# Smaller transfers for streamed weights: half a block each for Q, K, V and one row group each for the output weights

## The chip, the cores and the metric

The kernel runs on one core of one Trainium2 chip. The metric is device time in microseconds (us), the time of one execution as the device measures it. A profile of one execution and a trace of its instructions, semaphores and DMA packets belong to each kernel. In the lines of profiles PE is TensorE's matmuls, PEld its weight loads, DVE VectorE, ACT ScalarE, POOL GpSimd and SPq the queue of transfers that SyncE issues; L751 is line 751 of that run's kernel, so the same statement has another number in another run.

## The reference, cut to what matters

The program normalises x, runs layer A, adds it, normalises, runs layer B, adds it, and does all that once more. Layer A is a chain: 64 segments of 32 tokens, each of which starts from 8 memory rows that the segment before has produced. So the segments cannot be run side by side, and each one needs all four weight matrices again (32 heads of 192).

```python
for s in range(n_seg):                       # 2048 / 32 = 64 segments, in order
    xs = x[:, s * seg_len:(s + 1) * seg_len, :].copy()
    h = jnp.concatenate([mem, xs], axis=1)   # 8 memory rows + 32 tokens
    q = jnp.einsum('btd,dhe->bhte', h, Wq)
    k = jnp.einsum('btd,dhe->bhte', h, Wk)
    v = jnp.einsum('btd,dhe->bhte', h, Wv)
    scores = jnp.einsum('bhqe,bhke->bhqk', q, k) * scale
    # ... mask, softmax
    o = jnp.einsum('bhqk,bhke->bhqe', p, v)
    o = jnp.einsum('bhte,hed->btd', o, Wo)
    mem = o[:, :M, :].copy()                 # the next segment waits for this
    outs.append(o[:, M:, :])
```

## The kernel before

The kernel does not keep all weights in on-chip memory. A segment works in four rounds of 8 heads. Most Q, K, V blocks are resident (`res`); 10 blocks (3 of Q, 3 of K, 4 of V) have one slot each, which holds the block of round 0 or of round 3. The output weights of rounds 1 and 2 are resident (`wo_mid`), those of rounds 0 and 3 share `wo_end`. The order of rounds turns around from segment to segment, so that a slot is loaded only once a segment: as soon as the first round has read a slot, the block of the last round is fetched into it. All these loads are issued by SyncE, in program order.

```python
SLOTS = {"Q": 3, "K": 3, "V": 4}
PW = 1536                                     # columns of one block (8 heads x 192)

def load_slot(m, r, b):
    if holds.get((m, b)) != r:
        holds[m, b] = r
        nc.sync.dma_start(out=slot[m, b][:], in_=wview[m][:, b, PW * r:PW * r + PW])

def load_wo(r, into=None):
    t = into if into is not None else wo_end[:, :] if r in (0, 3) else wo_mid[:, 7680 * (r - 1):7680 * r]
    for k in range(4):
        nc.sync.dma_start(out=t[:, 1920 * k:1920 * k + 1920].rearrange("p (c m) -> p c m", m=640),
                          in_=wov[:, 12 * r + 3 * k:12 * r + 3 * k + 3, :])

def project(hT, ps, m, n, s, steps):          # round n of segment s: Q, K or V
    # ... for each block b of the round: four matmuls, then, in the first round:
        if n == 0 and b >= KC - ns:
            load_slot(m, order[NR - 1], b)    # the last round's block into the slot just read

def wo_round(W, r, OT, cs, first, last):      # output weights, 12 row groups c
    w = wo_end[:, :] if r in (0, 3) else wo_mid[:, 7680 * (r - 1):7680 * r]
    for c in cs:
        for g in range(4):
            nc.tensor.matmul(W[32 * g:32 * g + 32, 0:160], lhsT=OT[c // 6][:, c % 6, 8:40],
                             rhs=w[:, 640 * c + 160 * g:640 * c + 160 * g + 160], ...)

# in the chain, one segment s:
for n, r in enumerate(order):
    # ... project Q, K, V of round n; attention and wo_round of round n - 1
        if n == 1:
            load_wo(order[NR - 1])            # wo_end has been read by the first round
# ... after the four rounds:
keep_busy(idle, 4)
O, OT = attend(E, NR - 1)
keep_busy(idle, 2)
attend_rest(O, OT, otb, order[NR - 1])
wo_round(W, order[NR - 1], OT, range(12), False, True)   # the last round of output weights
keep_busy(idle, 3)
if s + 1 < NSEG:
    wt = ...                                  # VectorE: the memory rows out of W,
    nc.vector.transpose(out=wt[:, :, :], in_=W[:, 0:160].rearrange("p (j b) -> p b j", b=KC))
    nc.vector.tensor_copy(out=hT[:, :, 0:8], in_=wt[:, :, 0:8])   # input of the next segment
```

The softmax here doesn't subtract the row's maximum and nothing guards it: scores larger than these inputs give would overflow.

## Time and profile before

| | before |
|---|---|
| median of 3 runs | 4353.34 us (4347.0 to 4354.64) |
| TensorE busy, share of the span | 85% |
| layer A's two chains, 128 segments | 72% of the span, 24.5 us a segment (3135.6 / 128; the prediction's 24.9 divides by 126) |
| streamed a segment | 10 blocks of 384 KB and 4 pieces of 480 KB of output weights, 5.9 MB |
| TensorE's gaps after a fetch of its instructions, both chains | 274 us |

The prediction reads the main views. Three more are needed for the comparison later. First the order of time of SyncE's DMA queue in the segment that starts at 914.4 us (columns: start, length, engine and line, what goes where, how many in a row):

```profile
914.77 1.29 SPq L522 DMA_DIRECT2D wslotQ<-in_A_Wq_dram  x3
916.16 1.33 SPq L522 DMA_DIRECT2D wslotK<-in_A_Wk_dram  x3
917.59 2.02 SPq L522 DMA_DIRECT2D wslotV<-in_A_Wv_dram  x4
922.18 4.62 SPq L535 DMA_DIRECT2D wo_end<-in_A_Wo_dram  x4
```

The last output weights are issued 12.4 us into the segment (922.18 + 4.62 - 914.40).

Second, two of TensorE's groups (columns after the count: busy us, mean ns of one, then idle us just before them and what ended most of it):

```profile
L681 PE MATMUL ps_qk<-w_res,hT 128*32 128x384 bf16 x14336 | 804.8, 334 | 51.0 <-issue 48.0
...
L751 PE MATMUL ps_w<-wo_end,OT 128*32 128x160 bf16 x12288 | 290.5, 235 | 30.2 <-issue 15.9
```

The first are matmuls on resident weights, the second those on `wo_end`.

### The profile page before, as it was taken

The numbers are of one execution on the slowest core, as the hardware profiler recorded it, in microseconds if no ns is written. First come the engines' busy times: TensorE is split into PE (matmuls) and PEld (weight loads), VectorE is DVE, ScalarE is ACT, GpSimd is POOL, SyncE is SP. The second block draws the span as 40 slices with busy tenths as digits, with TensorE's granted clock in tenths as the row PEclk, the third lists the DMA queues.
The fourth block names the chain that finished last, engine by engine and source line by source line (L and its number), as shares of the span: only waits on it lengthen the run. The fifth ranks groups of instructions, "written<-read, shape, count | busy, mean of one in ns | idle before, by whom it ended". The sixth has DMA issues, their size and how long they took to land. (4 is left out here: it accounts for less than half of the span.)

```text
span 4350.8 us, 181511 instructions
## 1 busy us (share of the span) xinstructions
PE 3683.1 (85%) x77592; PEld 2223.0 (51%) x77608; DVE 2248.2 (52%) x5570; ACT 2024.4 (47%) x4973; POOL 1800.7 (41%) x5269
## 2 busy tenths in 40 slices
PE   5888888888888888869869888888888888888698
PEld 4645555555555555535347455555555555555353
DVE  4245555555555555536732455555555555554464
ACT  1245555555555555525412455555555555555152
POOL 1035555555555555430000355555555555553300
PEclk9989999999999999979989899999999999999798
DMA  7777777677677677740076876777777777777200
GB/s 258 214 264 271 254 274 259 247 268 257 247 261 262 239 275 258 273 126 1 31 248 193 280 269 240 273 259 258 276 250 271 251 262 271 252 266 272 84 1 25
DMA packets 613364, 983.28 MB, mean 226 GB/s; under 512 B 145098, under 2 KB 424650, under 8 KB 612554
## 3 DMA queue, kind: packets, MB, share of 16 engines
q1 hardware_dynamic: 459498, 861.74, 54.5%
q0 software_dynamic: 68224, 60.56, 4.6%
q10 hardware_dynamic: 84832, 49.36, 4.1%
q8 instruction: 609, 9.98, 0.9%
q14 instruction: 201, 1.65, 0.1%
HBM read 903.16 MB, written 68.16 MB: 223 GB/s over the span
## 5 line engine op out<-in xcount | busy, mean ns | idle before, releaser
L681 PEld LDWEIGHTS <-hT 128*32 128x32 bf16 x30720 | 785.9, 98 | 596.4 <-issue 217.7
L681 PE MATMUL ps_qk<-w_res,hT 128*32 128x384 bf16 x14336 | 804.8, 334 | 51.0 <-issue 48.0
L666 POOL DMA_DIRECT2D Vp<-vb x1024 | 539.1, 531 | 593.3 <-PE ps_o L733 518.5
L693 ACT ACTIVATE raw<-ps_qk 128x384 bf16<-128x384 f32 x1024 | 501.9, 490 | 547.4 <-PE ps_qk L681 529.4
L707 DVE CAST Vp<-ps_v 32x384 bf16<-32x384 f32 x1024 | 552.7, 540 | 36.3 <-PE ps_v L681 26.9
L751 PEld LDWEIGHTS <-OT 128*32 128x32 bf16 x24576 | 437.1, 99 | 234.0 <-issue 101.3
L698 DVE STREAM_TRANSPOSE QT<-raw 128x256 bf16<-128x256 bf16 x512 | 228.1, 445 | 613.9 <-ACT raw L693 604.1
L709 ACT ACTIVATE Vp<-ps_v 32x384 bf16<-32x384 f32 x1024 | 494.4, 483 | 64.0 <-PE ps_v L681 43.7
L658 POOL COPY QT<-kqb 128x64 bf16<-128x64 bf16 x512 | 121.8, 238 | 838.9 <-PE ps_s L722 403.5
L681 PE MATMUL ps_v<-w_res,hT 128*32 128x384 bf16 x6144 | 407.0, 330 | 29.7 <-issue 27.2
L786 DVE TENSOR_TENSOR E<-E,ps_s 128x160 bf16<-128x160 bf16 x512 | 164.6, 322 | 485.4 <-ACT ps_s L785 485.4
L751 PE MATMUL ps_w<-wo_mid,OT 128*32 128x160 bf16 x12288 | 351.1, 250 | 65.6 <-issue 63.0
L695 DVE STREAM_TRANSPOSE KT<-raw 128x384 bf16<-128x384 bf16 x512 | 296.1, 578 | 71.8 <-ACT raw L693 57.3
L739 ACT ACTIVATE OT<-ps_o 128x240 bf16<-128x240 f32 x512 | 190.0, 371 | 287.8 <-PE ps_o L733 275.7
L764 ACT ACTIVATE E<-ps_s 128x160 bf16<-128x160 f32 x512 | 155.7, 304 | 360.8 <-PE ps_s L722 356.6
L751 PE MATMUL ps_w<-wo_end,OT 128*32 128x160 bf16 x12288 | 290.5, 235 | 30.2 <-issue 15.9
L722 PE MATMUL ps_s<-QT,KT 128*40 128x40 bf16 (+1 forms) x6144 | 183.4, 189 | 127.9 <-DVE KT L695 63.3
L758 PE MATMUL ps_idle<-wo_mid,ident 128*128 128x384 bf16 x1152 | 270.0, 346 | 0.0
L681 PE MATMUL ps_v<-wslotV,hT 128*32 128x384 bf16 x4096 | 249.6, 332 | 22.8 <-issue 20.7
L743 DVE CAST OT<-ps_o 128x240 bf16<-128x240 f32 x512 | 195.9, 383 | 126.6 <-PE ps_o L733 122.9
L745 POOL COPY otb<-OT 128x48 bf16<-128x48 bf16 x1024 | 198.4, 231 | 125.1 <-ACT OT L739 117.3
L653 POOL DMA_DIRECT2D kqb<-kqb x256 | 148.0, 578 | 232.5 <-DMA vb<-wo_end 153.9
(148 smaller groups left out, 5485.4 us busy)
## 6 DMA issues: line engine op xcount, KB each, us to landing
wo_end<-in_A_Wo_dram SPq DMA_DIRECT2D x520, 480.0 KB
wslotV<-in_A_Wv_dram SPq DMA_DIRECT2D x536, 384.0 KB
wslotK<-in_A_Wk_dram SPq DMA_DIRECT2D x402, 384.0 KB
wslotQ<-in_A_Wq_dram SPq DMA_DIRECT2D x402, 384.0 KB
kqb<-wo_mid ACTq DMA_DIRECT2D x16, 1536.0 KB
kqb<-kqb POOLq DMA_DIRECT2D x256, 96.0 KB, 5.5
Vp<-vb POOLq DMA_DIRECT2D x1024, 14.0 KB, 4.8
vb<-wo_end ACTq DMA_DIRECT2D x128, 112.0 KB
```

Source lines behind the costliest of these rows:

```text
L666: nc.gpsimd.dma_start(out=Vs[n % 2][64 * G + 32:64 * G + 40, :], in_=self.vb_d[s, r, G])
L681: nc.tensor.matmul(o[32 * g:32 * g + 32, 0:384], lhsT=hT[:, b, :], rhs=rhs, start=(i == 0), stop=(i == KC - 1), tile_position=(0, 32 * g), ...
L693: nc.scalar.activation(out=raw[:], in_=ps[:, 0:384], func=ACT.Copy)
L695: nc.vector.transpose(out=KT[:, :, 0:32], in_=raw[:, :].rearrange("p (c j) -> p c j", j=32))
L698: nc.vector.transpose(out=qv[:, :, 0:4:3, 8:40], in_=rv[:, :, 0:3:2, :])
L707: nc.vector.tensor_copy(out=o, in_=i)
L709: nc.scalar.activation(out=o, in_=i, func=ACT.Copy)
L739: nc.scalar.activation(out=OT[0].rearrange("p c q -> p (c q)"), in_=O[0][:, 0:240], func=ACT.Copy)
L743: nc.vector.tensor_copy(out=OT[1].rearrange("p c q -> p (c q)"), in_=O[1][:, 0:240])
L745: nc.gpsimd.tensor_copy(out=otb[:, r, 6 * G:6 * G + 6, :], in_=OT[G][:, :, 0:8])
L751: nc.tensor.matmul(W[32 * g:32 * g + 32, 0:160], lhsT=OT[c // 6][:, c % 6, 8:40], rhs=w[:, 640 * c + 160 * g:640 * c + 160 * g + 160], sta ...
L758: nc.tensor.matmul(ps[:, 0:384], lhsT=self.ident[:, :], rhs=wo_mid[:, 0:384], start=True, stop=True, skip_group_check=True)
```

## The change

The intent: while weights stream, TensorE's own instructions are fetched late (a median 3.35 to 3.50 us after the start of the block before them, 0.78 where the queue is idle). With smaller transfers a fetch should wait for less; that was an estimate. Q, K, V blocks go out in two halves of 768 columns, the output weights in 12 pieces of one row group each. The bytes are the same. A segment issues 20 + 12 = 32 streamed transfers (192 and 160 KB) in place of 10 + 4 = 14 (384 and 480 KB).

```diff
             def load_slot(m, r, b):
                 if holds.get((m, b)) != r:
                     holds[m, b] = r
-                    nc.sync.dma_start(out=slot[m, b][:], in_=wview[m][:, b, PW * r:PW * r + PW])
+                    for h in range(2):
+                        nc.sync.dma_start(out=slot[m, b][:, 768 * h:768 * h + 768],
+                                          in_=wview[m][:, b, PW * r + 768 * h:PW * r + 768 * h + 768])
...
-                for k in range(4):
-                    nc.sync.dma_start(out=t[:, 1920 * k:1920 * k + 1920].rearrange("p (c m) -> p c m", m=640),
-                                      in_=wov[:, 12 * r + 3 * k:12 * r + 3 * k + 3, :])
+                for c in range(12):
+                    nc.sync.dma_start(out=t[:, 640 * c:640 * c + 640], in_=wov[:, 12 * r + c, :])
```

## The prediction

> **What bounds the kernel now.** I read the page first, then busy time by stretch, then TensorE's order of time, then SyncE's, then the packet records of the trace.
>
> The page: TensorE is busy 85% of the span and no other engine passes 52%; queue q1 (SyncE's weight loads) fills over half of the DMA engines' time; queue q8 carries instructions.
>
> ```profile
> PE   5888888888888888869869888888888888888698
> ...
> q1 hardware_dynamic: 459498, 861.74, 54.5%
> ...
> q8 instruction: 609, 9.98, 0.9%
> ```
>
> The two layers A (272 to 1847 us and 2443 to 4003 us, two times 64 segments) hold 72% of the span, and streamed weights move in them, so one segment is the unit to read: 24.9 us on average. Busy time by stretch of the segment from 914.4 us on (columns: stretch, its length, busy us of each engine with counts, granted clock, DMA share, GB/s):
>
> ```profile
> 914.40:916.90 2.50, 2.50 (x64) 1.67 (x68) 0.92 (x3) 1.03 (x3) 2.25 (x6) 1.00 0.52 106
> 920.90:924.90 4.00, 2.05 (x70) 1.38 (x67) 2.04 (x5) 1.95 (x6) 1.37 (x4) 1.00 1.04 406
> 924.90:928.90 4.00, 3.59 (x48) 1.97 (x47) 1.19 (x4) 0.98 (x2) 0.86 (x4) 0.59 1.04 396
> 936.20:939.60 3.40, 3.23 (x83) 1.72 (x76) 1.53 (x5) 1.39 (x5) 1.86 (x7) 1.00 0.02 5
> ```
>
> The weights keep all 16 DMA engines full (share 1.04) from some 2.5 to 18 us of the segment and are gone for the rest. That is slack, so bandwidth is not the bound. But while they run TensorE loses half of a stretch (2.05 of 4 us), and in the next one its clock falls to 0.59. TensorE in order of time there:
>
> ```profile
> 922.93 0.34 PE L681 MATMUL ps_qk<-w_res,hT 128*32 128x384 bf16 x4
> 925.31 2.78 PE L681 MATMUL ps_qk<-w_res,hT 128*32 128x384 bf16 x36 [2.04 <-issue]
> 927.83 1.22 PE L681 MATMUL ps_v<-w_res,hT 128*32 128x384 bf16 x12
> ```
>
> TensorE stands 2.04 us in front of resident weights, on "issue": it waits for nothing that a semaphore tells. The packet records say for what. The 609 packets of q8 are 16,384 bytes each, one for each 256 TensorE instructions, and stalls come at instruction numbers a multiple of 256 apart (28097, 29121, 29377 and so on). In both chains 213 gaps over 0.5 us, 275 us in all (6.3% of the kernel), end 1.24 to 1.58 us (5th to 95th percentile, median 1.42) after an instruction packet has landed. **The bound is TensorE, waiting for its own instructions** behind the weights. From the start of one block of 256 to the fetch of the next passes a median 0.78 us where q1 is idle, 3.35 us under 3,072-byte packets and 3.50 us under 1,280-byte ones. The fetch takes 0.95, the tail 1.42; blocks in the loaded part last 4.6 to 4.9 us without their stall. So a delay to about 2.2 us is free and one of 3.5 us costs some 1.2. Of fetches starting 10 to 14 us into a segment 96% stall; in its first 6 us none, in its last 4 us one in 72.
>
> Waits for the weights themselves are small, as the table of waits shows:
>
> ```profile
> PE ps_qk L681 <- DMA wslotQ<-in_A_Wq_dram: 11.9, 6, 6.0
> ...
> PE ps_w L751 <- DMA wo_end<-in_A_Wo_dram: 4.6, 5, 1.3
> ```
>
> [...] a fetch does not get in after one 121 ns record; it waits 2.6 us longer than in quiet, as if behind about three whole transfers' shares. [...] half-clock spells last 3.4 us, and 52 of the 53 in the chains (201 us) have a gap over 1 us in the 4 us ahead of them. [...]
>
> **The change part by part.** TensorE, VectorE and ScalarE keep every compute instruction. Q, K and V blocks (384 KB, 128 packets of 3,072 B) become two transfers of 192 KB in 1,536 B packets; output weights go from 4 transfers of 480 KB to 12 of 160 KB, still in 1,280 B packets. A segment issues 10 + 4 = 14 streamed transfers now, 20 + 12 = 32 after.
>
> *DMA time.* A 3,072 B packet takes a median 121 ns, a 1,536 B one (GpSimd's queue) 65, taken as 64. Per segment: 10 x 128 x (128 - 121) ns / 16 engines = 0.6 us, and 18 more completion packets per engine at 9 ns = 0.2 us. The stream ends near 19 us instead of 18. Last-round slots are read from about 17 us and output weights from about 23 us, in order of issue; Q, K and V slots go first. Off the path: 0.
>
> *SyncE's issue.* Its rows, with min/median/max ns:
>
> ```profile
> L535 SPq DMA_DIRECT2D wo_end<-in_A_Wo_dram x520: 367/406/2555, 236.5 to 3986.7; - x174
> L522 SPq DMA_DIRECT2D wslotQ<-in_A_Wq_dram x402: 327/382/1965, 53.2 to 3977.6; - x134
> ```
>
> An issue takes 0.38 us, and successive ones stand 0.475 us apart with their semaphore waits. 32 x 0.475 = 15.2 us of 24.9: it fits. More to the point, it paces the stream: 196,608 B / 0.475 us = 414 GB/s and 163,840 / 0.475 = 345 GB/s, against the 380 to 400 that the DMA engines drain. Now 393 KB go out per issue, so SyncE runs ahead: at block starts 4 to 12 us into the segment I count 2.1 to 2.4 MB issued and not moved. Where that count is 0.6 MB the delay is 1.57 us, where it is zero 0.7 to 1.1. The program has eight hardware completion semaphores in turn, so at most eight transfers are out: 3.1 MB now, 1.5 MB (Q, K, V) or 1.3 MB after, and pacing should keep it near 1 MB.
>
> *Fetch delay after.* If a fetch waits for about three transfers: extra 3 x 8 x 64 ns = 1.5 us for Q, K, V and 3 x 8 x 55 = 1.3 for output weights, on 0.8: 2.1 to 2.3 us. If it waits for bytes outstanding: 1 MB lies between 1.57 and 3.5 us, say 2.4. Laying each delay on the measured blocks of the loaded part, stalls of all would be 234 us at 3.2, 122 at 2.8, 35 at 2.4 and 2 at 2.0. I take 45 left of 274: **229 us of stall go**. A fit of segment length on stall and half-clock time has 0.80 us per us of stall (other engines use some of it to catch up) and 0.34 per us of half clock. 229 x 0.80 = 183. If 80% of the 201 us of half clock go, 0.34 x 161 = 55. Sum 238 us, so 4115 us. I give back 25 for the next wait in line (keys' transposes, the small loads of memory rows) and end at 4140.
>
> **The rivals.** (a) The delay follows bytes or descriptors in a fixed queue, not transfers: then 3.5 stays 2.8 or more, at most half of the stalls go, and the time is 4220 to 4350. For it: delay is almost alike under 3,072 B and 1,280 B packets. Against it: it falls with the amount outstanding. (b) More issues and smaller packets make SyncE or the DMA engines late, and TensorE waits for slots: 4350 to 4450. Against it: 15.2 us of issue and some 17 of transfer in a segment of 24.9. (c) TensorE loses a stall and meets another wait as long: DVE and ACT are busy some 52 to 54% in the chains, and TensorE's waits for keys are 63 us in all, so little of it. (d) Small GpSimd loads gain too: values from memory land in a median 1.38 us in quiet and 4.83 under load; this helps slightly.
>
> **Range and chances.** Best case, the fit's segment with neither stall nor half clock, 22.5 us: 126 x 2.4 = 300 us less, 4050. Rival (a) gives the upper end, 4290. A gain of 2% needs a third of the stalls and their half-clock spells gone. Faster 0.83, same 0.14, slower 0.03.
>
> **What would show it right or wrong.** Right: TensorE's "issue" gaps in the loaded part mostly under 0.5 us; clock in the chains above its 0.97; a segment near 23 us; q1's bytes the same with its share two or three points of DMA time up; no new waits for slots. Wrong: gaps of 1 to 2 us at multiples of 256 instructions as before (rival a), or TensorE waiting on slot tiles (rival b). The prediction is most exposed at the fetch delay, which I infer from a pattern and not from a record of what the fetch waits behind.

## More of the kernel before

The transfers take eight completion semaphores in turn (in the trace the numbers 101 to 103 and 113 to 117). None of the 1,790 streamed issues that I could match with a landing starts before the transfer that had its semaphore last has landed whole (63 ns after it at the least), and at none are more than seven others out: at most eight of SyncE's transfers are out at a time.

Third, VectorE's table of waits, its row for `wt`, the instruction that ends each segment (total us, times, longest):

```profile
DVE wt L866 <- PE ps_w L751: 133.9, 126, 1.7
```

VectorE stands 1.06 us in front of the segment's last matmul (133.9 / 126). That row is a gauge of the last round: it grows by whatever delays it once VectorE is already there.

## The result, and the profile after

The changed kernel takes 4353.14 us, median of 4 runs (4348.15 to 4363.39), against 4353.2 (4347.0 to 4354.64) for the kernel before in the same session. The ratio is 1.0007 with a 95% interval of 0.999 to 1.0023: the same time. The prediction was 4140.

The page of the changed kernel, the same lines:

```profile
PE   4888998998989898769869888988999989997698
...
q1 hardware_dynamic: 669866, 861.89, 60.3%
...
q8 instruction: 609, 9.98, 0.9%
```

TensorE is busier (more nines), yet no faster as a whole. q1 moves the same bytes, but its packets now take 60.3% of the DMA engines' time, not 54.5: 5.8 points, where the prediction allowed two or three.

The same two groups of TensorE:

```profile
L682 PE MATMUL ps_qk<-w_res,hT 128*32 128x384 bf16 x14336 | 800.4, 337 | 2.1 <-issue 1.6
...
L752 PE MATMUL ps_w<-wo_end,OT 128*32 128x160 bf16 x12288 | 365.4, 236 | 152.1 <-DMA wo_end<-in_A_Wo_dram 112.9
```

In front of resident weights the idle time falls from 51.0 to 2.1 us: the instruction fetches come in time (the fetch delay under Q, K, V is 2.12 us, and was 3.35). In front of the matmuls on `wo_end` it rises from 30.2 to 152.1, and now a DMA ends it. The busy column of that group also grows, 290.5 to 365.4 us at an unchanged mean of 236 ns for one: short waits between matmuls hide in the busy time of a run of them. Together (152.1 - 30.2) + (365.4 - 290.5) = 197 us.

The tables of waits say the same, for TensorE and for VectorE:

```profile
PE ps_w L752 <- DMA wo_end<-in_A_Wo_dram: 112.9, 194, 2.7
```

```profile
DVE wt L867 <- PE ps_w L752: 342.4, 126, 5.7
```

The gauge goes from 133.9 to 342.4 us: 208.5 us more, 1.65 us for each of 126 segments.

One segment shows how. SyncE's queue in the segment that starts at 826.84 us:

```profile
827.23 3.66 SPq L523 DMA_DIRECT2D wslotQ<-in_A_Wq_dram  x6
830.98 2.76 SPq L523 DMA_DIRECT2D wslotK<-in_A_Wk_dram  x6
833.84 5.12 SPq L523 DMA_DIRECT2D wslotV<-in_A_Wv_dram  x8
839.53 7.60 SPq L537 DMA_DIRECT2D wo_end<-in_A_Wo_dram  x12
```

The last piece is issued 20.3 us into the segment (839.53 + 7.60 - 826.84), where it was 12.4 before. TensorE at the end of that segment:

```profile
847.26 1.05 PE L752 MATMUL ps_w<-wo_end,OT 128*32 128x160 bf16 x32
848.46 1.04 PE L752 MATMUL ps_w<-wo_end,OT 128*32 128x160 bf16 x12 [0.15 <-DMA wo_end<-in_A_Wo_dram]
849.66 0.25 PE L752 MATMUL ps_w<-wo_end,OT 128*32 128x160 bf16 x4 [0.16 <-DMA wo_end<-in_A_Wo_dram]
```

TensorE starts the last round 20.4 us into the segment, earlier than before, and follows the pieces as they land: 2.6 us for 48 matmuls that take some 1.0 us when the weights are there. Busy time by stretch in that segment (columns as in the prediction: stretch, its length, busy us of PE, PEld, DVE, ACT and POOL with counts, granted clock, DMA share, GB/s):

```profile
833.50:837.50 4.00, 3.69 (x114) 2.48 (x113) 2.46 (x7) 2.60 (x7) 2.08 (x8) 1.00 1.05 357
837.50:841.50 4.00, 3.46 (x112) 2.25 (x110) 2.58 (x7) 2.30 (x7) 2.78 (x9) 1.00 1.06 377
841.50:845.50 4.00, 4.00 (x126) 2.50 (x118) 2.81 (x7) 2.51 (x7) 1.86 (x8) 1.00 0.90 276
845.50:847.20 1.70, 1.67 (x34) 0.69 (x22) 0.91 (x3) 1.19 (x4) 0.39 (x2) 1.00 0.88 281
847.20:849.90 2.70, 1.92 (x49) 1.09 (x50) 0.08 (x1) 0.01 (x1) 1.98 (x5) 1.00 0.55 179
```

In the middle of the segment TensorE now works 3.69, 3.46 and 4.00 of 4 us at full clock, where the prediction's lines had 2.05 of 4 and a clock of 0.59. The DMA engines are as full there at first (1.05 and 1.06, before 1.04), but move 357 and 377 GB/s (last column) at the places where the kernel before moved 406 and 396. Then, from 14.7 us of the segment, they fall to 276 GB/s at 0.90, and the stream is still running at the segment's end. There VectorE and ScalarE have nothing to do (0.08 and 0.01): everything waits for the last weights.

On the mean of the 128 segments, read from the trace's records (time within the segment):

| | before | after |
|---|---|---|
| last piece of V lands | 14.7 us | 16.3 us |
| last output weights land | 19.9 us | 23.5 us |
| TensorE starts the last round | 23.4 us | 21.5 us |
| that round takes | 0.96 us | 2.61 us |
| TensorE's gaps after an instruction fetch, both chains | 274 us | 50 us |
| half-clock spells in the chains (granted clock 0.5, 3.4 us for most) | 53 (201 us) | 51 (195 us) |

TensorE reaches the last round 1.92 us sooner, 246 us over 128 segments, and loses 1.65 us of it, 211 us, in that round. The chains as wholes come out 20.5 and 6.9 us shorter in the profiled executions. Outside them some of that goes too: SyncE is still issuing the last segment's pieces, and the loads of the output stage stand behind them in its program, so the gap between each chain and that stage grows from 2.8 to 13.8 and from 2.4 to 12.2 us. With a chain's borders at its first projection and its last output matmul, the stretch ahead of the first chain takes 7.3 us more, the one between the chains 14.4 and the one behind the second 11.1. Sum: -27.4 + 32.8 = +5.4 us, the difference between the two profiled spans (4356.2 and 4350.8).

### Why the stream is slow

The queue is held by its eight completion semaphores: none of the 4,126 streamed issues matched in this trace starts before the landing of the transfer that had its semaphore last (16 ns after it at the least), and none with more than seven others out. From about the 12th to the 26th transfer of a segment, each issue comes 0.1 to 0.6 us after the landing of the transfer eight before it, by which that one's semaphore is free again (means: the 17th is issued at 9.69 us, the 9th has landed at 9.57; the 20th at 11.77, the 12th at 11.54). Eight transfers out were 3.1 MB before; they are 1.57 MB (Q, K, V) or 1.31 MB (output weights) now. A transfer of 192 KB lands every 0.69 us, 285 GB/s, one of 160 KB every 0.61 us, 268 GB/s; before, the pace was 330 to 378 GB/s.

Each transfer raises its semaphore sixteen times, and the profile's page counts 16 DMA engines. For a piece of output weights the first of the sixteen steps comes 1.87 us after the end of its issue, the median one at 2.42 and the last at 3.59 us. Read as one step for each engine, the last engine finishes 1.2 us after the median one, and no issue on this semaphore starts before the last step. That the engines that finish early then have too little queued is argued from this and tested in e6.

### The profile page after: what moved, and what is told of

Same layout as the page of the kernel before. It is cut to its first block, busy times and chain, and to the rows that moved or that the text cites. A ratio compares the mean times of both kernels' runs of the same rounds, so it can differ in the third digit from the quotient of the medians. Undisturbed runs are those within 1.5% of the kernel's fastest.

```text
span 4356.2 us, 185503 instructions
## 1 busy us (share of the span) xinstructions
PE 3755.0 (86%) x77592; PEld 2222.9 (51%) x77608; DVE 2246.9 (52%) x5570; ACT 2024.2 (46%) x4973; POOL 1797.8 (41%) x5269
## 3 DMA queue, kind: packets, MB, share of 16 engines
q1 hardware_dynamic: 669866, 861.89, 60.3%
## 4 chain that ended last, share of the span: by engine, by line
PE 52%; DMA 23%; DVE 10%; ACT 6%; issue 6%; POOL 3%; SPq 1%; ACTq 0%; POOLq 0%; DVEq 0%
PE ps_qk L682 13%; DMA wo_end<-in_A_Wo_dram 12%; PE ps_w L752 8%; PE ps_v L682 5%; DMA kqb<-kqb 4%; PE ps_pre L594 3%; PE ps_s L723 3%; DVE KT L696 2%; ACT raw L694 2%; PE ps_s L780 2%; PE ps_qk L342 2%; PE pp L892 2%; DVE QT L699 2%; PE ps_o L734 2%; DMA wslotV<-in_A_Wv_dram 2%
## 5 line engine op out<-in xcount | busy, mean ns | idle before, releaser
L752 PE MATMUL ps_w<-wo_end,OT 128*32 128x160 bf16 x12288 | 365.4, 236 | 152.1 <-DMA wo_end<-in_A_Wo_dram 112.9
L682 PE MATMUL ps_v<-w_res,hT 128*32 128x384 bf16 x6144 | 394.6, 329 | 13.3 <-issue 13.2
L752 PE MATMUL ps_w<-wo_mid,OT 128*32 128x160 bf16 x12288 | 322.0, 238 | 15.2 <-issue 14.6
L696 DVE STREAM_TRANSPOSE KT<-raw 128x384 bf16<-128x384 bf16 x512 | 296.0, 578 | 38.5 <-ACT raw L694 23.3
L682 PE MATMUL ps_v<-wslotV,hT 128*32 128x384 bf16 x4096 | 258.5, 336 | 10.2 <-DMA wslotV<-in_A_Wv_dram 6.6
L744 DVE CAST OT<-ps_o 128x240 bf16<-128x240 f32 x512 | 194.7, 380 | 69.6 <-PE ps_o L734 60.3
L734 PEld LDWEIGHTS <-Vp 40*128 40x128 bf16 x8192 | 137.9, 93 | 175.2 <-issue 111.3
```

Source lines behind the costliest of these rows:

```text
L682: nc.tensor.matmul(o[32 * g:32 * g + 32, 0:384], lhsT=hT[:, b, :], rhs=rhs, start=(i == 0), stop=(i == KC - 1), tile_position=(0, 32 * g), ...
L696: nc.vector.transpose(out=KT[:, :, 0:32], in_=raw[:, :].rearrange("p (c j) -> p c j", j=32))
L734: nc.tensor.matmul(O[G][:, o0:o0 + 40], lhsT=Vs[n % 2][64 * G:64 * G + 40, 448 * x + k:448 * x + k + 128], rhs=E[64 * G:64 * G + 40, 80 * ...
L744: nc.vector.tensor_copy(out=OT[1].rearrange("p c q -> p (c q)"), in_=O[1][:, 0:240])
```

## The experiments

Two questions: is the wait for the last weights what took the gain (theory L in the expectations: the eight semaphores hold fewer bytes out, and the last weights land late), and is the slow stream due to that cap on bytes outstanding, or to the smaller packets and pieces as such? The expectations say in their own words what each theory gives. Ratios are against the kernel before in the same rounds. The table holds all runs; the edits follow. "Fetch gaps" are TensorE's gaps after an instruction fetch in both chains, "lands" the mean landing of the last output weights and "reached" the mean time at which TensorE starts on them, all three my readings of the records; `wt` is VectorE's gauge.

| run | us, median | ratio (95%) | fetch gaps | lands | reached | `wt` wait |
|---|---|---|---|---|---|---|
| before | 4353.2 | 1 | 274 | 19.9 | 23.4 | 133.9 |
| after | 4353.14 | 1.0007 (0.999-1.0023) | 50 | 23.5 | 21.5 | 342.4 |
| e1 last round on resident weights | 4128.18 | 0.953 (0.9503-0.9558) | 48 | 23.7, unread | 21.1 | 149.4 |
| e2 Q, K, V halves alone | 4359.25 | 1.0054 (1.0025-1.0083) | 170 | 22.9 | 22.2 | 270.8 |
| e3 output weights in 12 alone | 4268.3 | 0.9846 (0.9819-0.9873) | 199 | 21.0 | 22.7 | 133.7 |
| e4 halves by rows | 4805.9 | 1.1084 (1.1059-1.1108) | 74 | 26.6 | 26.3 | 177.1 |
| e5 output weights in one | 4331.96 (one run) | none | 259 | 19.9 | 23.3 | 133.4 |
| e6 before, with fillers | 4352.89 | 1.0043 (1.0012-1.0075) | 93 | 23.2 | 21.8 | 314.9 |
| e7 V halves, output in 12 | 4242.07 | 0.978 (0.9756-0.9804) | 110 | 22.3 | 21.8 | 213.9 |
| e8 K, V halves, output in 12 | 4236.7 | 0.9779 (0.9738-0.982) | 54 | 22.4 | 21.2 | 256.2 |
| e9 K, V halves, output in 8 | 4221.06 | 0.9727 (0.9707-0.9747) | 137 | 21.7 | 21.9 | 183.9 |
| e10 K, V halves, output in 6 | 4240.5 | 0.9768 (0.9747-0.979) | 168 | 21.6 | 22.0 | 193.2 |

The kernel before was run again in each session: 4339.84 us beside e1 to e4, 4338.47 beside e5 to e8, 4343.93 beside e9 and e10 (medians of 7).

### e1_nowait: the last round reads resident weights

On the changed kernel. All transfers stay; the last round reads another round's output weights, which are resident. Its output is wrong, which doesn't matter for the time.

```diff
-                w = wo_end[:, :] if r in (0, 3) else wo_mid[:, 7680 * (r - 1):7680 * r]
+                w = wo_end[:, :] if r in (0, 3) and not last else wo_mid[:, 7680 * (r // 2):7680 * (r // 2) + 7680]
```

> Wrong result on purpose: the changed kernel, in which the output-weight matmuls of a segment's last round read resident weights, so that they wait for no streamed transfer; every transfer still goes out. Theory L (late weights: the small transfers did free TensorE from some 220 us of instruction-fetch stalls, and the output weights, which now land at 23.5 us of a segment while TensorE is there at 21.5, took it back): the last round's output matmuls take 1.0 us again instead of 2.6, a segment falls from 24.6 to about 23.0 us, and the time to 4150 (4100 to 4200). Rival R (no gain was there to take back: with the fetch stalls gone another engine or the clock holds TensorE to the same pace): the wait moves to the next segment's reads and the time stays at 4320 to 4360.

4128.18 us (4107.29 to 4141.85), 4.7% less than before. VectorE's and TensorE's tables of waits:

```profile
DVE wt L867 <- PE ps_w L752: 149.4, 126, 2.5
```

```profile
PE ps_w L752 <- DMA wo_end<-in_A_Wo_dram: 3.7, 9, 1.0
```

The gauge is back (149.4 against 133.9), though the weights still land at 23.7 us. The half-clock spells go too: 6 in the chains (20 us) in place of 51. So the wait for the last output weights (112.9 us of TensorE's time in the changed kernel's table, 3.7 here) took the gain, and the half-clock spells of the changed kernel go with it. Without it the kernel is 212 us faster than before (4339.84 - 4128.18).

### e2_qkv_halves and e3_wo_twelve: each part alone

e2 keeps the halves of Q, K, V and has the output weights in 4 transfers again. e3 keeps the 12 transfers and has whole Q, K, V blocks. Each undoes one part of the diff shown above.

> One part of the change alone: halves for Q, K and V, output weights in 4 transfers as before. Theory L: fetch delay falls to about 2.1 us in the first half of a segment and stays near 3.5 under the output weights; the last output weights land near 21.5 us of a segment, just as TensorE comes to them; about 100 to 150 us of the stalls go for good and the time is 4200 to 4280. Rival S (the number of issues on SyncE has little to do with the lateness, the smaller packets have all of it): they land as late as in the changed kernel, 23 us or later, and the time is 4320 to 4380.

> The other part alone: Q, K, V blocks whole, output weights in 12 transfers. Theory L: fetch delay stays near 3.4 us until the Q, K, V blocks have drained (some 14 us of the segment) and falls to under 2 us after; last landing near 20.5 us, no wait for it; about a third of the stalls go and the time is 4240 to 4300. Rival S (packets are what is slow): also no late landing here, so 4240 to 4300 as well; if instead it is 4340 or more with late output weights, twelve issues in a row are the cause by themselves.

e2: 4359.25 us, 0.5% slower than before. The expectation of theory L was missed, in time and in landing (22.9 us): large final transfers do not make up for the slow start, since V's last piece already lands at 16.5 us in place of 14.7, and the gauge shows 270.8. Halved Q, K, V blocks alone suffice to make the last weights late. By its number this run fits the rival that blames small packets as well as a cap on Q, K and V; e6 below tells them apart.

e3: 4268.3 us, 1.5% faster, as expected, but by both theories, so it does not tell them apart. The fetch delay under output weights falls from a median 3.50 us to 1.90, under Q, K, V it stays (3.25 against 3.35), so 75 of 274 us of gaps go. The weights land at 21.0, TensorE comes at 22.7, and the gauge does not move:

```profile
DVE wt L865 <- PE ps_w L750: 133.7, 126, 1.8
```

So the parts do not add: one gives -1.5%, the other +0.5%, both +0.1%. Both draw on the same slack, the time between the landing of the last weights and their use: e3 leaves 1.7 us of it, the whole change has none.

### e4_row_halves: halves by rows, with the old packets

The changed kernel with Q, K, V blocks halved by rows: 64 rows of 3,072 bytes each.

```diff
-                        nc.sync.dma_start(out=slot[m, b][:, 768 * h:768 * h + 768],
-                                          in_=wview[m][:, b, PW * r + 768 * h:PW * r + 768 * h + 768])
+                        nc.sync.dma_start(out=slot[m, b][64 * h:64 * h + 64, :],
+                                          in_=wview[m][64 * h:64 * h + 64, b, PW * r:PW * r + PW])
```

> The changed kernel with Q, K, V blocks split by rows instead of columns: the same 32 transfers of the same bytes in a segment, but packets of 3,072 bytes instead of 1,536. If the time per packet makes the stream late (rival S): packet time falls from 160 x 73 ns to 80 x 130 ns an engine and segment, 1.3 us less, output weights land near 22 us and the time is 4180 to 4260. If the round trips of eight outstanding transfers and SyncE's issues do (theory L, as I hold it): the landing moves by under 0.7 us and the time is 4290 to 4360.

4805.9 us, 10.8% slower: both theories missed it. The same 3,072-byte packets now take a mean 187 ns in place of 134, the last piece of V lands at 20.9 us, and TensorE waits for V itself:

```profile
PE ps_v L682 <- DMA wslotV<-in_A_Wv_dram: 392.7, 359, 2.4
```

As a test of the packet's size the run is spoilt, since it changes which rows lie in a transfer, and the packets got slower for a reason that no run here isolates. What it does show: halves of rows are far worse than halves of columns.

### e5_wo_one: one transfer of 2.0 MB

The kernel before, with the output weights of a round in one transfer (12 x 163,840 bytes are 1.97 MB; the expectation says 1.9).

```diff
-                for k in range(4):
-                    nc.sync.dma_start(out=t[:, 1920 * k:1920 * k + 1920].rearrange("p (c m) -> p c m", m=640),
-                                      in_=wov[:, 12 * r + 3 * k:12 * r + 3 * k + 3, :])
+                nc.sync.dma_start(out=t[:, 0:7680].rearrange("p (c m) -> p c m", m=640), in_=wov[:, 12 * r:12 * r + 12, :])
```

> The kernel before with the output weights in one transfer of 1.9 MB. If the fetch delay beyond quiet (0.8 us) goes on in proportion to the transfer's size (2.45 us at 384 KB, 3.0 at 480), it is limited only by what is left of the transfer, up to 5 us: fetch delays of 4 us and more while it runs, and a time of 4370 to 4450. If it follows the bytes outstanding, which are the same as before: 3.5 us and 4330 to 4365.

One run, 4331.96 us, inside the range of the kernel before (4330.07 to 4351.88). The fetch delay under output weights is 3.47 us, as with 4 transfers (3.50), and as expected if it follows the bytes outstanding. A fetch does not wait for a number of whole transfers: these are four times as large. The prediction had left open which of the two it is.

### e6_lane_fill: the kernel before with half of its bytes outstanding

The kernel before, its transfers and packets unchanged, with a tiny one (8 bytes a row) after each streamed one. The tiny ones take every second completion semaphore, so that only four large transfers can be out (the issues below bear it out: a large one comes 0.2 us after the landing of the large one four before it).

```diff
+            pads = wres.tile([P, 64], BF16, name="pads")
+            def fill():
+                if not unread:
+                    nc.sync.dma_start(out=pads[:, 4 * (fills[0] % 16):4 * (fills[0] % 16) + 4], in_=wview["Q"][:, 0, 0:4])
+                    fills[0] += 1
...
                     nc.sync.dma_start(out=slot[m, b][:], in_=wview[m][:, b, PW * r:PW * r + PW])
+                    fill()               # likewise after each transfer of load_wo (cut)
```

> The kernel before, with an 8-byte-per-row transfer after each streamed one in the segments; each takes one of the eight completion semaphores, so only four big transfers are out at a time, 1.5 MB as in the changed kernel, while the transfers themselves stay at 384 and 480 KB. Two questions. What a fetch waits behind: if a fixed number of transfers, the delay stays near 3.3 us; if bytes outstanding, it falls to about 2.1. What slows the stream of the changed kernel: if the cap on what is outstanding does (theory L), the last output weights land 2 to 3 us later than in the kernel before, 22 us or more, and the time is 4340 to 4420; if the shorter transfers' cost on the DMA engines does (packets of the same size took 62 ns instead of 56 there), the landing stays under 20.8 us and the time at 4330 to 4370.

4352.89 us, 0.4% slower, and the trace looks like that of the changed kernel. The time lies in the ranges of both theories; the landing tells them apart. The fetch delay under Q, K, V falls to 1.96 us (before 3.35, after 2.12) and the fetch gaps to 93 us. (Under the output weights, where four large transfers are 2.0 MB as before, it falls less: to some 2.6 us in a second reading of the records, which gives 3.7 before.) The last weights land at 23.2 us; TensorE reaches them at 21.8 and waits. TensorE's group on `wo_end` and VectorE's gauge:

```profile
L761 PE MATMUL ps_w<-wo_end,OT 128*32 128x160 bf16 x12288 | 326.2, 236 | 166.8 <-DMA wo_end<-in_A_Wo_dram 131.2
```

```profile
DVE wt L876 <- PE ps_w L761: 314.9, 126, 5.2
```

SyncE's queue, in the middle of one segment:

```profile
959.58 0.38 SPq L530 DMA_DIRECT2D wslotV<-in_A_Wv_dram  x1
960.00 0.44 SPq L520 DMA_DIRECT2D pads<-in_A_Wq_dram  x1
960.70 0.33 SPq L530 DMA_DIRECT2D wslotV<-in_A_Wv_dram  x1
```

On the mean each large issue there comes 0.2 us after the landing of the large one four before it (8.67 after 8.48, 10.13 after 9.99, 11.52 after 11.34 us). So half the bytes outstanding bring both the early fetch and the late stream, with packets of the old size. The fillers are not quite free, and that has to come off: their packets take 1.0 us of each DMA engine a segment. (That they delay the stream by no more than this is assumed.) That leaves some 2.2 of the 3.3 us of later landing for the cap. Of these, 1.1 us are that the same packets take longer (3,072 bytes 142 ns against 134, 1,280 bytes 61 against 56), the rest that the engines stand idle for moments (busy 0.93 to 1.03 from 10 us to 20 us of the segment; 1.02 to 1.06 before, while its stream ran).

Read the same way, the changed kernel's 3.6 us later landing holds 1.6 us of longer packets (1,536 bytes 73 ns where half a 3,072-byte packet is 67; 1,280 bytes 63 against 56), 0.2 us of more completion packets (4 bytes; 38,848 more of them in the queue for 2,428 more issues in the whole program, 16 a transfer, at a mean 9 ns), and the rest idle moments and the spread of the last transfer. The small packet as such may own a part of the 1.6, but probably not most: e6 has 1.1 without it. In all three kernels the median packet of a size takes the same time (121, 65 and 55 ns for 3,072, 1,536 and 1,280 bytes); what grows is a tail. The slowest hundredth of the 1,280-byte packets in the chains begins at 55 ns before, at 201 in e6 and at 291 in the changed kernel.

### e7_v_halves and e8_kv_halves: where in the segment to be small

The changed kernel with Q and K whole (e7) or only Q whole (e8), so that the stream starts with much outstanding while instruction fetches in this part are still in time.

```diff
-                    for h in range(2):
-                        nc.sync.dma_start(out=slot[m, b][:, 768 * h:768 * h + 768],
-                                          in_=wview[m][:, b, PW * r + 768 * h:PW * r + 768 * h + 768])
+                    for h in range(2 if m in "KV" else 1):          # e7: in "V"
+                        wd = 768 if m in "KV" else PW
+                        nc.sync.dma_start(out=slot[m, b][:, wd * h:wd * h + wd],
+                                          in_=wview[m][:, b, PW * r + wd * h:PW * r + wd * h + wd])
```

> Output weights in 12 and V blocks in halves, Q and K whole. Theory L: the stalls of fetches asked for 8 to 12 us into a segment (96 of the 200 us left with the 12 alone) go, the last landing moves from 21.0 to about 21.8 us, just in time: 4180 to 4240. If stalls shift to output-weight waits instead: 4260 to 4300.

> As the run with V halves, and K blocks in halves too. Theory L: 77 us more of stalls go, but the last landing moves to about 22.6 us and TensorE, which would be there at 21.6, waits a microsecond of it: 4190 to 4280, not better than V halves alone by more than 20 us.

4242.07 and 4236.7 us, both 2.2% faster than before (by the record's threshold of 2% both are unclear, since their intervals reach across it). e7 misses theory L's range by 2 us, with a landing 0.5 us later than expected; e8 lies in its range. In e7 V lands as early as before (14.9 us), in e8 at 15.2; the last weights land at 22.3 and 22.4, still after TensorE's 21.8 and 21.2. e8 has fewer fetch gaps (54 us against 110) and a larger gauge (256.2 against 213.9): one is traded for the other.

### e9_kv_wo_eight and e10_kv_wo_six: a faster end

e8 with larger first pieces of output weights: 2, 2, 2, 2, 1, 1, 1, 1 row groups (e9) or six pieces of 2 (e10).

```diff
-                for c in range(12):
-                    nc.sync.dma_start(out=t[:, 640 * c:640 * c + 640], in_=wov[:, 12 * r + c, :])
+                c = 0
+                for k in (3, 3, 3, 3) if into is not None else (2, 2, 2, 2, 1, 1, 1, 1):     # e10: (2, 2, 2, 2, 2, 2)
+                    nc.sync.dma_start(out=t[:, 640 * c:640 * (c + k)].rearrange("p (c m) -> p c m", m=640),
+                                      in_=wov[:, 12 * r + c:12 * r + c + k, :])
+                    c += k
```

> A version to beat both: Q whole, K and V in halves, output weights in 8 transfers (four of 320 KB, then four of 160 KB), and those for the last stage in 4 as before. If bytes outstanding set both the fetch delay and the stream's pace, a little more outstanding at the first output weights brings the last landing from 22.4 to about 21.8 us of a segment while the delay under them stays below 2.5 us; with 8 us less a layer at the end of the chain: 4170 to 4225. If the landing does not move: 4215 to 4245.

> The same with the output weights in 6 transfers of 320 KB. Bytes outstanding: last landing near 21.3 us, no wait for it, but fetch delays under the output weights of 2.5 to 2.8 us cost 30 to 80 us of stall; 4170 to 4240, and not better than eight transfers by more than 20 us. If the delay went with the number of transfers ahead instead, it would be 2.8 us or more and the time 4240 or more.

e9: 4221.06 us (4215.95 to 4226.49), 2.7% faster, the best of all and correct. Its weights land at 21.7 us, just before TensorE comes at 21.9. VectorE's and TensorE's waits:

```profile
DVE wt L871 <- PE ps_w L756: 183.9, 126, 4.1
```

```profile
PE ps_w L756 <- DMA wo_end<-in_A_Wo_dram: 12.1, 33, 1.9
```

TensorE's wait for the DMA is down to 12.1 us from 112.9. The time was within what was expected, but not for the whole of the reason: the fetch delay under output weights is 3.17 us, not below 2.5, so 137 us of fetch gaps are back. e10 (4240.5 us) lands at the same 21.6 us with a delay of 3.35 and is no better than e8, a near miss of its expectation. Time and delay are even those named there for a delay that goes with the number of transfers ahead. But six pieces of 320 KB are 2.0 MB, which can all be out at once like the four pieces before, so that bytes outstanding, worked out so, give the delay of before (3.50) too. e10 does not separate the two; e5 and e6 do. Both show again that the two quantities move together: each gain in the stream's pace is paid in the fetch delay.

### What stays open

- Why packets of half-row transfers take 187 ns (e4).
- Why 1,280-byte packets take 63 ns in short transfers and 56 in long ones. e6 ties part of it to the bytes outstanding; what makes a packet last longer then, no run tells.
- Whether SyncE's own issue time is a limit. In the changed kernel the last six issues of output weights come 0.5 to 0.9 us after the landing that frees their semaphore, later than the 0.1 to 0.6 of the issues before them. e6, with 28 issues a segment, has no small pieces and is late too, but a part of the delay of the last pieces may be SyncE's.
- What exactly holds a fetch back.

## Why the prediction was wrong, point by point

**The bound named was real.** e1 takes the new wait away, and 48 us of fetch gaps are left where 45 were predicted; that kernel's gain is 212 us, where the prediction's sum after its deduction was 213. That they agree to 1 us is partly luck: e1's chains came out 277 us shorter, and some 32 us of it were lost outside them (245 between the profiled spans). The fetch delay of 2.1 to 2.4 us came out as 2.12 (under Q, K, V) and 1.79 (under output weights).

**The step that failed is the one on DMA time**: "The stream ends near 19 us instead of 18", and after it "Off the path: 0." It counted longer packets and completion packets, 0.8 us in all, on engines assumed to be as full as before. The stream's end moved by 3.6 us, from 19.9 to 23.5: 1.6 of longer packets, 0.2 of completion packets, and 1.8 of moments without work and of the last transfer's spread, for which the prediction had no term. Its start was misread too: about 18 us is where the mean share of the DMA engines falls, but the last weights landed, to the last step of their semaphores, at 19.9. And it took the packets' medians, which did not move; the means did. The text held the missing piece. It states that at most eight transfers are out, "3.1 MB now, 1.5 MB (Q, K, V) or 1.3 MB after", and uses it only for the fetch delay. It also counted on SyncE's pace of issue to keep only about 1 MB out; from the 12th transfer of a segment on, the eight semaphores set the pace instead. Less outstanding also left the engines idle for moments: in e6, with packets of the old size, they were busy 0.93 to 1.03 from 10 to 20 us of the segment, where the kernel before had 1.02 to 1.06. The same halving that let fetches in (3.35 to 2.12 us under Q, K, V) slowed the stream from 330 to 378 GB/s to some 268 to 285.

**The second half of that step was the moving target.** The prediction compared the new stream end with the old time of use, "about 23 us". A TensorE that loses less comes earlier, at 21.5 us. The slack was 3.5 us (23.4 - 19.9); the stream used up 3.6 of it and TensorE's own gain another 1.9. Either alone would have fit or nearly so; together they miss by 2.0 us (23.5 - 21.5), of which the mean round lost 1.65. Over 128 segments that is 211 us: the whole gain.

**Rival (b) was right in kind.** It foresaw that DMA engines come late and TensorE waits, and was put aside with "15.2 us of issue and some 17 of transfer in a segment of 24.9". That argument adds up how much work there is; it does not ask when it is due, nor that issue and transfer hold each other up through the eight semaphores (issues 0.1 to 0.6 us after the landing eight before). Its time (4350 to 4450) begins where the result lies. The views that it asked for, TensorE waiting on streamed tiles, are just what the profile shows, on `wo_end` and not on the Q, K, V slots.

**Rival (a)** held in one half: the delay follows bytes outstanding, not a count of transfers (3.47 us with one transfer of 2.0 MB in e5, where four had 3.50; 1.96 with half the bytes out in e6, where all had 3.35). Its other half, a fixed queue, and with it its consequence did not hold, since the bytes outstanding fall with the change (3.1 MB to 1.57 and 1.31).

**The half clock**: 161 of 201 us were to go; 195 stayed, though the fetch gaps went. e1 shows 20. With the new wait once a segment the spells stay (51), without it they go (6). That they would go with the fetch gaps was the prediction's estimate, from the gap over 1 us in the 4 us ahead of 52 of the 53. How much idle time starts a spell is not shown: in the 3.4 us before each of the 53 of the kernel before, its matmuls leave 1.2 to 2.7 us free (median 1.8).

**The rate of gain** per us of stall, 0.80, was too low rather than too high: 224 us less of fetch gaps brought TensorE to its last round 246 us sooner, summed over the segments. e1 says the same: 0.80 x 226 + 0.34 x 181 = 242 us by the fit, 277 in the chains.

**What would have shown it beforehand**: the two times within a segment, the landing of the last streamed tile (19.9) and its first use (23.4), both in the trace before. The change had to keep the first below the second, after the second had moved down by the hoped-for gain of about 1.7 us a segment (213 / 128).

## What to carry to other kernels

SyncE's queue had at most eight transfers out here, so the size of a transfer set the bytes outstanding (3.1 MB before, 1.57 and 1.31 after), and with them both the pace of the stream (330 to 378 GB/s, then 268 to 285) and the delay of instruction fetches under Q, K, V (3.35 us, then 2.12; 1.96 in e6 with the old packets): the smaller transfer bought one with the other. Where a trace shows the same, before such a change compare the landing of the last streamed tile with the time at which it will be needed if the gain comes true, not with the time at which it is needed now. Then choose the size by place: large where there is nothing to be disturbed, small where a fetch is due (e9: 2.7% faster than the kernel before, with which the changed kernel ties).
